# Four layouts for the split operands of a feed-forward: x high and u low in pieces with gaps, x low and u high shifted along their rows

## The chip, the cores and the metric

The kernel runs on one NeuronCore of a Trainium2 chip. Its engines work side by side and meet at semaphores: TensorE (PE, with its weight loads shown apart as PEld), VectorE (DVE), ScalarE (ACT), GpSimd (POOL) and SyncE (SP, which here issues all DMAs). The metric is the device time of one launch in microseconds; lower is better.

## The reference

A linear attention with quadratic features, and behind it a feed-forward with a squared ReLU. Cut to what is computed:

```python
batch, n_heads, seq, head_dim, r = 4, 4, 1088, 32, 8        # all float32

def phi(x):                                       # 64 features from 32 dims
    a = np.einsum('rd,bhsd->bhsr', S1, x)
    b = np.einsum('rd,bhsd->bhsr', S2, x)
    return np.einsum('bhsi,bhsj->bhsij', a, b).reshape(*x.shape[:-1], r * r)
q_p, k_p = phi(q), phi(k)
kv = np.einsum('bhsf,bhsd->bhfd', k_p, v)
z = np.sum(k_p, axis=2)
attn = np.einsum('bhsf,bhfd->bhsd', q_p, kv) / (np.einsum('bhsf,bhf->bhs', q_p, z)[..., None] + 1e-06)

x = attn.transpose(0, 2, 1, 3).reshape(4352, 128)           # tokens x d_model
h = x @ w_in                                                # 128 -> 2048
g = s * np.maximum(h, 0.0) ** 2 + b
out = g @ w_out                                             # 2048 -> 128
```

## The kernel before

The 4352 tokens are the columns of everything: x stands in SBUF as 128 features (partitions) by tokens, and it is cut into nine tiles, one of 256 tokens and eight of 512 (`TILES`, line 26). For each tile the feed-forward runs over eight pairs of 128-wide blocks of the 2048 hidden units (`ffn(t, jp)`, line 527). A pair is two products into one two-bank PSUM tile `hp`, a ReLU and a square on ScalarE (`square`, line 470) that leave `u` in SBUF, and two products that add to the tile's output `ops`.

A float32 product at full precision is made in three passes. Each operand is split in a high part, its value rounded to the type float32r, and a low part, the rest. The weights are split once (`split_weights`, line 448): `wih`, `wil` for w_in and `woh`, `wol` for w_out. The moving operands are split tile by tile: `split_x` (line 257) makes `xh` and `xl` from a tile's attention output, `split_u` (line 477) makes `uh` and `ul` from `u`. In both, the high part is one copy that rounds (line 146, on VectorE or ScalarE by the list `ON_DVE`), and the low part is one VectorE subtraction that reads the value and the high part (lines 263 and 482). A product is then low weights times high stream, high weights times low stream, high times high, in this order, in one PSUM bank (`product`, line 486; each call is a weight load and a matmul that streams 512 columns of the moving operand past the weights). So x high is streamed twice for each block and x low once, u high twice and u low once. The last pair of the last tile makes its second product in two halves of 256 columns, into `psa`.

The first tile of 256 tokens does not split its operands (`first_ffn`, line 494): it multiplies plain float32 tiles. `SPLIT_0 = ((), ())` (line 35) leaves the code for splitting it unused.

The four split tiles lie in SBUF as plain rows of each partition, one float32r after the other: `xh` and `xl` are 512 columns, `uh` and `ul` two times 512. They come from pools with two buffers (`p2`: xh, xl, u) and three (`p3`: uh, ul).

All work is written as generators, one for each load, weight piece, attention tile and feed-forward pair, and a list of names, `ORDER` (line 34), says which of them makes its next step. Each engine runs its instructions in the order in which this list issues them, and nothing is moved afterwards. The change doesn't touch the list.

Of the kernel before, what the change touches and what calls it, by code (L numbers as in the profile page):

```python
# [10 lines left out]
F32R = mybir.dt.float32r  # L11
# [4 lines left out]
ALU = mybir.AluOpType  # L16
# [3 lines left out]
P = 128  # L20
# [4 lines left out]
NMAX = 512  # L25
# [6 lines left out]
VT = 38 * LINE  # L32
EPS = 1e-6
ORDER = """Ls s s z z z z Lq1 Lk0 Lk0 Lv0 Lq0 z Lk0 Lv0 Lw0 z z z z z z z Lv0 Lk1 q1 sr q1 Lcst Lw2 q1 Lk1 Lq2 s k0 k0 k0 k0 p w0 w0 p k0 k0 k0 k0 k0 k0 k0 k0 k0 k1 w0 p k0 k0 k1 w2 w2 k0 k0 z z z z k1 f f f f w0 f Lw3 Lw1 Lv1 q1 Lq3 Lv1 q2 q2 f Lk2 Lw4 Lk2 q1 q1 q1 q1 q2 f k1 f 00 01 k1 k1 w2 w1 w1 w1 w1 w2 00 w3 q3 w3 q3 00 w4 w4 w3 w0 k1 k1 01 k1 k2 02 00 w4 k2 k1 w3 01 w0 k2 w4 k2 k2 02 02 k2 01 03 03 03 Lw6 Lv2 Lv2 Lw5 q2 05 02 04 w1 05 w6 w6 w4 05 q1 n1 n1 n1 n1 n1 w2 03 k2 k2 q3 Lk3 Lw7 Lk3 q2 q2 q2 q2 Lq4 q3 w5 w6 w5 k2 k2 n1 k3 w7 w3 w7 04 04 w6 06 w5 w5 05 n1 n1 06 06 w7 k3 w7 07 04 n1 k1 10 07 07 w2 w4 w1 06 10 10 k3 w5 q2 k1 k1 11 07 11 10 n2 w5 n2 n2 n2 q3 12 10 11 11 11 12 12 n2 n2 k3 q4 13 10 15 11 q3 q3 q3 12 12 q4 n2 n2 w6 w7 13 07 w3 13 15 13 w6 k3 k3 13 12 14 15 15 q3 q4 n2 Lq5 Lv3 Lq6 n2 Lq7 q4 n2 n2 Lv3 17 n3 n3 n3 14 14 n3 14 15 14 q4 q4 n3 q4 n3 07 q4 16 13 15 q7 q5 w7 n2 n2 n2 16 16 q5 16 16 q7 17 17 17 n3 n3 17 14 k2 k3 k3 q5 q5 n3 n3 n3 n3 20 20 16 21 k2 20 k3 21 21 17 23 24 q4 20 20 k2 k3 23 23 21 21 24 n4 n4 n4 n4 23 23 22 20 21 25 n4 24 22 17 22 n4 q5 q5 q5 q5 24 24 23 n4 n4 n3 22 22 n3 25 25 25 n3 25 24 22 26 27 25 q6 q5 q6 n4 n4 n4 q6 26 27 26 26 26 27 n5 n5 n5 n5 27 27 30 30 34 34 34 30 26 34 31 32 27 30 n5 n5 n5 30 34 31 31 32 31 31 n4 q6 17 q6 q6 q6 q6 30 34 33 32 32 32 33 33 33 33 n4 n5 q6 31 36 k3 k3 n4 k3 36 36 36 36 32 33 35 37 n4 35 35 37 27 q7 q7 n5 n5 35 35 n6 n6 n6 37 n6 37 37 q7 Lq8 n5 n6 n5 27 n6 36 40 40 42 35 37 41 40 40 42 40 n5 n6 q7 q7 q7 37 42 41 41 42 42 n6 44 40 43 42 n5 41 41 44 44 43 43 43 n5 44 44 q7 43 45 46 41 q8 q8 n7 46 46 46 46 n7 n7 45 n7 44 43 50 45 50 45 50 45 47 46 q8 n6 q8 n6 n7 n7 50 n7 q8 n6 q8 n6 37 47 47 50 47 n7 47 52 45 51 52 51 52 51 51 50 53 47 52 52 53 n6 51 53 54 54 53 53 52 51 56 54 54 53 55 54 56 56 n6 n6 47 56 55 55 55 q8 q8 56 q8 n7 n7 n7 n7 n7 55 57 54 56 60 n8 47 57 57 n8 60 n8 n8 57 60 57 62 55 61 57 n8 n8 n8 60 62 62 62 60 n8 63 62 60 62 61 57 61 61 61 63 n7 63 64 65 61 64 64 63 n7 63 64 65 65 65 64 66 63 65 66 66 n8 n8 n8 n8 57 66 66 64 67 70 67 67 70 70 67 67 65 71 71 70 70 71 72 66 67 n8 71 71 n8 72 72 72 72 73 74 73 70 71 72 75 74 74 73 73 73 74 74 n8 75 75 75 75 76 73 77 76 76 77 77 81 74 80 76 76 76 75 77 77 81 81 80 80 81 81 82 77 83 82 67 67 80 80 82 83 83 82 82 84 80 81 85 84 84 83 83 85 85 86 82 84 84 87 83 84 85 85 86 77 86 86 86 85 86 87 87 77 86 87 87 87 87 87 87 87 87"""
SPLIT_0 = ((), ())
DIRECT = (1,)
ON_DVE = """a6 a8 b03 b06 b10 b30 b35 d2 d3 d4 k31 n1 n2 n3 n6 n7 n8 u10 u12 u16 u20 u21 u22 u23 u24 u26 u30 u31 u32 u33 u34 u35 u37 u41 u42 u44 u45 u50 u52 u53 u57 u61 u63 u66 u67 u70 u71 u73 u74 u75 u76 u77 u80 u82 u83 u84 u85 u86 u87 w0 w1 w2 w5 w7 x2 x4 x6""".split()
CMASK, CS, CB, CID = 0, 2, 3, 4
# [20 lines left out]
def attn_ffn_kernel(ctx: ExitStack, tc: tile.TileContext, qT, kT, vp, s64, cst, w_in, w_out, outT):  # L59
    nc = tc.nc  # L60
# [3 lines left out]
    p2 = ctx.enter_context(tc.tile_pool(name="p2", bufs=2))  # L64
# [7 lines left out]
    def f32(ap):  # L72
        return ap.bitcast(F32)
# [71 lines left out]
    def copy(key, out, in_):  # L145
        (nc.vector.tensor_copy if key in ON_DVE else nc.scalar.copy)(out=out, in_=in_)  # L146
# [109 lines left out]

    def split_x(t, x):
        N = tiles[t][1] - tiles[t][0]
        xh = p2.tile([P, NMAX], F32R, name="xh")
        xl = p2.tile([P, NMAX], F32R, name="xl")  # L260
        copy(f"x{t}", xh[:, :N], x[:, :N])
        yield
        nc.vector.tensor_tensor(out=xl[:, :N], in0=x[:, :N], in1=f32(xh[:, :N]), op=ALU.subtract)
        xhl[t] = (xh, xl)
        yield

# [29 lines left out]
    def first_attend(t):  # L296
        N = tiles[t][1] - tiles[t][0]
        pq, st = qfeat.pop(t), kv_st[0]
        C = N // P
        nd = ps_h.tile([P, 2, 512], F32, name="hp")  # L300
        for c in range(C):
            for g in range(2):
                nc.tensor.matmul(nd[:, 0, 4 * c + 2 * g:4 * c + 2 * g + 2], pq[:, g, c * P:(c + 1) * P],
                                 st[:, 1 + g, :2], start=(c == 0 and g == 0),
                                 stop=(c == C - 1 and g == 1), skip_group_check=True)
        yield
        rc = const.tile([P, LINE], F32, name="rc0")[:, :4 * C].rearrange("p (c h) -> p c h", h=4)
        nc.vector.tensor_scalar(out=rc, in0=nd[:, 0, :4 * C].rearrange("p (c h) -> p c h", h=4), scalar1=EPS,
                                scalar2=None, op0=ALU.add)
        yield  # L310
        nc.vector.reciprocal(out=rc, in_=rc)
        yield
        rx = const.tile([P, C, P], F32, name="rx")
        for c in range(C):
            nc.vector.tensor_copy(out=rx[:, c].rearrange("p (g d j) -> p g d j", g=2, j=2),
                                  in_=rc[:, c].rearrange("p (g j) -> p g j", g=2).unsqueeze(2).broadcast_to([P, 2, D, 2]))
        yield
        numerators(nd[:, 1, :N], st, pq, slice(0, N))
        yield
        num = const.tile([P, N], F32, name="num0")  # L320
        nc.scalar.copy(out=num, in_=nd[:, 1, :N])
        yield
        rp = ps_a.tile([P, 512], F32, name="psa")
        for c in range(C):
            nc.tensor.matmul(rp[:, c * P:(c + 1) * P], rx[:, c], ident,  # L325
                             start=(c == 0), stop=(c == C - 1), skip_group_check=True)
        yield
        x = const.tile([P, N], F32, name="x0")
        nc.vector.tensor_tensor(out=x, in0=num, in1=rp[:, :N], op=ALU.mult)
        x_first.append(x)  # L330
        yield
        if any(SPLIT_0):
            yield from split_x(t, x)

    def qfeatures(t):
        N = tiles[t][1] - tiles[t][0]
# [138 lines left out]
        return u  # L475

    def split_u(key, u, N):
        uh = p3.tile([P, 2, NMAX], F32R, name="uh")
        copy(key, uh[:, :, :N], u[:, :, :N])
        yield  # L480
        ul = p3.tile([P, 2, NMAX], F32R, name="ul")
        nc.vector.tensor_tensor(out=ul[:, :, :N], in0=u[:, :, :N], in1=f32(uh[:, :, :N]), op=ALU.subtract)  # L482
        yield
        return uh, ul

# [8 lines left out]
    def first_ffn(jp):  # L494
        N = TILES[0]
        hp = ps_h.tile([P, 2, 512], F32, name="hp")
        for i in range(2):
            c, c24 = columns(2 * jp + i)
            if jp in SPLIT_0[0]:
                xh, xl = (x[:, :N] for x in xhl[0])  # L500
                terms = ((wil[:, c], xh), (wih[:, c], xl), (wih[:, c], xh))
            else:
                terms = ((w24[jp // 2, 0][c24], x_first[0]),)
            product(hp[:, i, :N], terms)
        yield
        u = yield from square(hp, N)

        nc.scalar.copy(out=u[:, :, N:N + 2], in_=b_col.unsqueeze(2).broadcast_to([P, 2, 2]))
        yield
        W = N + 2  # L510
        if jp in SPLIT_0[1]:
            uh, ul = yield from split_u(f"u0{jp}", u, W)
        if jp == 0:
            o_ps[0] = ps_o.tile([P, 512], F32, name="ops")
        for i in range(2):
            c, c24 = columns(2 * jp + i)
            if jp in SPLIT_0[1]:
                terms = ((wol[:, c], uh[:, i, :W]), (woh[:, c], ul[:, i, :W]), (woh[:, c], uh[:, i, :W]))
            else:
                terms = ((w24[jp // 2, 1][c24], u[:, i, :W]),)  # L520
            product(o_ps[0][:, :W], terms, jp == i == 0, jp == NPAIR - 1 and i == 1)
        yield
        if jp == NPAIR - 1:
            nc.scalar.copy(out=bias, in_=o_ps[0][:, N:N + 1])
            yield from finish(0, o_ps[0], slice(0, N))

    def ffn(t, jp):
        N = tiles[t][1] - tiles[t][0]
        xh, xl = (x[:, :N] for x in xhl[t])
        hp = ps_h.tile([P, 2, 512], F32, name="hp")  # L530
        for i in range(2):
            c, _ = columns(2 * jp + i)
# [10 lines left out]
        for a in range(2 if final else 1):  # L543
# [2 lines left out]
            o = ps_a.tile([P, 512], F32, name="psa") if final else o_ps[t]  # L546
            for i in range(2):
                c, _ = columns(2 * jp + i)
                product(o[:, :M], ((wol[:, c], uh[:, i, s]), (woh[:, c], ul[:, i, s]), (woh[:, c], uh[:, i, s])),
                        i == 0 and (jp == 0 or final), i == 1 and (last or final))  # L550
            yield
            if final:
# [80 lines left out]
```

## Time and profile before

| what | value |
|---|---|
| median of two runs | 241.64 us (241.63 to 241.65) |
| the profiled execution's own time | 241.36 us |
| its span, first to last instruction | 239.3 us |
| PE busy | 234.9 us (98%) |
| PE weight loads busy | 185.0 us (77%) |
| ACT busy | 190.4 us (80%) |
| DVE busy | 168.6 us (70%) |
| POOL busy | 3.0 us (1%) |
| mean granted TensorE clock | 1.000 |

The profiled execution is 0.28 us shorter than the median, and 2.1 us of it lie outside the span. A matmul's recorded duration reaches past the start of the next one, because matmuls are pipelined and their ends are modelled; how fast they follow each other is read from their starts, or from the chain of waits, which counts each only once. Weight loads are shown beside the matmuls and overlap them.

### The profile page before, as it was taken

Reading aid. Unit: us, or ns where it says so; the run is one execution under the profiler, and the core shown is the slowest. Engines: PE = TensorE matmul, PEld = TensorE weight load, DVE = VectorE, ACT = ScalarE, POOL = GpSimd, SP = SyncE. Lnnn points to the kernel's source line nnn. Section 1 sums busy time; section 2 is a strip of 40 time slices with the busy share of each in tenths; the row PEclk is TensorE's granted clock in tenths of the full one; section 3 lists DMA queues with packets and bytes.
Section 4 is the critical chain, followed back from the end, with each engine's and each line's share of the span. In section 5 each row is a group of like instructions: output and inputs, shape, how many; then the busy total and the mean of one; then the engine's idle time right before and its main releaser. Section 6 shows DMA issues by size and latency. Waiting matters only on the chain.

```text
span 239.3 us, 3880 instructions
## 1 busy us (share of the span) xinstructions
PE 234.9 (98%) x1481; PEld 185.0 (77%) x1482; DVE 168.6 (70%) x224; ACT 190.4 (80%) x238; POOL 3.0 (1%) x16
## 2 busy tenths in 40 slices
PE   8999999999999999999999999999999999999994
PEld 3978869778678786788788778887688888788883
DVE  1677979988777684579868865667655682965973
ACT  3348779799767887968789969999998989697971
POOL 3010000000000000000000000000000000000000
PEclk9999999999999999999999999999999999999999
DMA  6999985057641050252054017002002000000011
GB/s 172 361 405 318 322 297 176 3 133 257 178 135 44 4 169 29 89 130 70 1 184 129 1 53 223 15 0 88 1 4 88 0 0 0 3 0 31 13 45 44
DMA packets 15541, 25.21 MB, mean 105 GB/s; under 512 B 3492, under 2 KB 6052, under 8 KB 15524
## 3 DMA queue, kind: packets, MB, share of 16 engines
q1 hardware_dynamic: 15524, 24.98, 32.6%
q8 instruction: 11, 0.18, 0.3%
q14 instruction: 6, 0.05, 0.1%
HBM read 21.59 MB, written 3.33 MB: 104 GB/s over the span
## 4 chain that ended last, share of the span: by engine, by line
PE 97%; DVE 1%; issue 0%
PE hp L488 40%; PE ops L488 39%; PE psa L221 4%; PE psa L199 3%; PE psa L250 3%; PE ops L578 2%; PE psa L342 2%; PE psa L407 1%; PE hp L286 1%; PE psa L488 1%; DVE ph L206 1%; PE psa L418 0%; PE psa L325 0%; PE hp L250 0%; PE psa L234 0%; DVE ot L553 0%
## 5 line engine op out<-in xcount | busy, mean ns | idle before, releaser
L482 DVE TENSOR_TENSOR ul<-u,uh 128x1024 fp32r<-128x1024 f32 x64 | 78.2, 1224 | 21.4 <-ACT uh L146 19.9
L472 ACT ACTIVATE u<-hp 128x1024 f32<-128x1024 f32 (+1 forms) x72 | 70.2, 976 | 23.3 <-PE hp L488 12.1
L474 ACT ACTIVATE u<-u 128x1024 f32<-128x1024 f32 (+1 forms) x72 | 72.5, 1013 | 1.7
L488 PE MATMUL hp<-xh,wil 128*128 128x512 f32 x128 | 51.1, 399 | 0.0
L488 PE MATMUL hp<-xl,wih 128*128 128x512 f32 x128 | 49.9, 390 | 0.0
L488 PE MATMUL hp<-xh,wih 128*128 128x512 f32 x128 | 49.9, 390 | 0.0
L488 PE MATMUL ops<-uh,wol 128*128 128x512 f32 x126 | 49.5, 393 | 0.0
L488 PE MATMUL ops<-ul,woh 128*128 128x512 f32 x126 | 49.1, 390 | 0.0
L488 PE MATMUL ops<-uh,woh 128*128 128x512 f32 x126 | 49.1, 389 | 0.0
L146 DVE CAST uh<-u 128x1024 fp32r<-128x1024 f32 x42 | 29.0, 692 | 24.9 <-ACT u L474 22.0
L488 PEld LDWEIGHTS hp<-xh,wil 128*128 128x128 f32 x128 | 24.0, 188 | 7.4 <-issue 1.4
L488 PEld LDWEIGHTS ops<-uh,wol 128*128 128x128 f32 x126 | 23.7, 188 | 5.8 <-issue 0.8
L488 PEld LDWEIGHTS hp<-xh,wih 128*128 128x128 f32 x128 | 24.0, 188 | 5.2
L488 PEld LDWEIGHTS hp<-xl,wih 128*128 128x128 f32 x128 | 24.0, 188 | 4.7
L488 PEld LDWEIGHTS ops<-uh,woh 128*128 128x128 f32 x126 | 23.7, 188 | 5.0
L488 PEld LDWEIGHTS ops<-ul,woh 128*128 128x128 f32 x126 | 23.6, 188 | 4.8
L146 ACT CAST uh<-u 128x1024 fp32r<-128x1024 f32 x22 | 23.1, 1049 | 0.6
L206 DVE TENSOR_TENSOR ph<-psa,bk 128x768 f32<-128x768 f32 (+2 forms) x9 | 11.0, 1221 | 3.9 <-ACT bk L146 3.8
L360 DVE TENSOR_TENSOR pq<-pq,br 128x1024 f32<-128x1024 f32 x8 | 9.7, 1211 | 0.0
L199 PEld LDWEIGHTS psa<-sk,kt 128*128 128x128 f32 x72 | 9.0, 191 | 0.9 <-issue 0.4
L199 PE MATMUL psa<-sk,kt 128*128 128x64 f32 x72 | 9.3, 274 | 0.0
L127 ACT ACTIVATE w<-raw 128x512 f32<-128x512 f32 x8 | 5.4, 679 | 4.9 <-DMA raw<-w_in 4.8
(88 smaller groups left out, 176.5 us busy)
## 6 DMA issues: line engine op xcount, KB each, us to landing
pq<-qd SPq DMA_DIRECT2D x16, 256.0 KB
br<-qd SPq DMA_DIRECT2D x16, 256.0 KB
qt<-qT SPq DMA_DIRECT2D x8, 256.0 KB
raw<-w_in SPq DMA_DIRECT2D x4, 512.0 KB
raw<-w_out SPq DMA_DIRECT2D x4, 512.0 KB
rr<-rd SPq DMA_DIRECT2D x14, 128.0 KB
outT<-ot SPq DMA_DIRECT2D x7, 256.0 KB
qd<-abq SPq DMA_DIRECT2D x16, 64.0 KB
```

Source lines behind the costliest of these rows:

```text
L127: nc.scalar.activation(out=out, in_=high.bitcast(F32), func=AF.Abs, scale=2.0 ** -112)
L146: (nc.vector.tensor_copy if key in ON_DVE else nc.scalar.copy)(out=out, in_=in_)
L199: nc.tensor.matmul(av[:, :, i, :], kt[:, (c0 + i) * P:(c0 + i + 1) * P], sk.rearrange("p (w x) -> p w x", w=2), start=(i == 0), stop=(i == ...
L206: nc.vector.tensor_tensor(out=ph[:, c0:c0 + n].rearrange("p c h i x -> p (c h) i x"), in0=a[:, :n * 32].rearrange("p (g y) -> p g y", y=R) ...
L221: nc.tensor.matmul(kvp[64 * g:64 * g + VW, 64 * j:64 * j + 64], v_in[b][:, c, h], ph[:, c, h].rearrange("p i x -> p (i x)"), start=(c == 0 ...
L250: nc.tensor.matmul(out[r:r + 32], st[:, 3 * g, r % 64:r % 64 + 32], pq[:, g, cols], start=True, stop=True, skip_group_check=True)
L342: nc.tensor.matmul(ab[r:r + 32, :M], sq[:, r % 64:r % 64 + 32], qT_t[t][:, a * M:(a + 1) * M], start=True, stop=True, skip_group_check=True)
L360: nc.vector.tensor_tensor(out=pq[:, :, :N], in0=pq[:, :, :N], in1=br[:, :, :N], op=ALU.mult)
L472: nc.scalar.activation(out=u[:, :, :N], in_=hp[:, :, :N], func=AF.Relu)
L474: nc.scalar.activation(out=u[:, :, :N], in_=u[:, :, :N], func=AF.Square)
L482: nc.vector.tensor_tensor(out=ul[:, :, :N], in0=u[:, :, :N], in1=f32(uh[:, :, :N]), op=ALU.subtract)
L488: nc.tensor.matmul(out, w, x, start=(first and k == 0), stop=(last and k == len(terms) - 1), skip_group_check=True)
```

## The change

Each of the four streams gets a layout of its own in SBUF; their values, the instructions and their order stay.

- `xh`: the tile is twice as long, 64 groups of two times 8 elements, and the second 8 of each group are used. The stream is 64 pieces of 32 bytes with 32 bytes between them, and it begins 32 bytes into the tile.
- `xl`: a plain row that begins 4 elements (16 bytes) into a tile 32 elements longer.
- `uh`: two plain rows of 512 that begin 12 elements (48 bytes) into rows of 544.
- `ul`: two rows of 16 groups of two times 32 elements, of which the first 32 are used: pieces of 128 bytes with 128 bytes between them.

The access patterns of the copies that write the high parts, of the subtractions that read these and write the low parts, and of the matmuls that stream all four follow; no DMA reads or writes these tiles. In `ffn` a stream's slice of the last pair counts `ul` in groups of 32. The unused `SPLIT_0` code goes.

```diff
     def split_x(t, x):
         N = tiles[t][1] - tiles[t][0]
-        xh = p2.tile([P, NMAX], F32R, name="xh")
-        xl = p2.tile([P, NMAX], F32R, name="xl")
-        copy(f"x{t}", xh[:, :N], x[:, :N])
-        yield
-        nc.vector.tensor_tensor(out=xl[:, :N], in0=x[:, :N], in1=f32(xh[:, :N]), op=ALU.subtract)
+
+        xh = p2.tile([P, NMAX // 8, 2, 8], F32R, name="xh")[:, :, 1]
+        xl = p2.tile([P, NMAX + 32], F32R, name="xl")[:, 4:NMAX + 4]
+        copy(f"x{t}", xh, x.rearrange("p (g c) -> p g c", c=8))
+        yield
+        nc.vector.tensor_tensor(out=xl.rearrange("p (g c) -> p g c", c=8), in0=x.rearrange("p (g c) -> p g c", c=8),
+                                in1=f32(xh), op=ALU.subtract)
         xhl[t] = (xh, xl)
         yield
...
     def split_u(key, u, N):
-        uh = p3.tile([P, 2, NMAX], F32R, name="uh")
-        copy(key, uh[:, :, :N], u[:, :, :N])
-        yield
-        ul = p3.tile([P, 2, NMAX], F32R, name="ul")
-        nc.vector.tensor_tensor(out=ul[:, :, :N], in0=u[:, :, :N], in1=f32(uh[:, :, :N]), op=ALU.subtract)
+
+        uh = p3.tile([P, 2, NMAX + 32], F32R, name="uh")[:, :, 12:NMAX + 12]
+        copy(key, uh, u)
+        yield
+        ul = p3.tile([P, 2, NMAX // 32, 2, 32], F32R, name="ul")[:, :, :, 0]
+        nc.vector.tensor_tensor(out=ul, in0=u.rearrange("p i (g c) -> p i g c", c=32),
+                                in1=f32(uh).rearrange("p i (g c) -> p i g c", c=32), op=ALU.subtract)
         yield
         return uh, ul
...
     def ffn(t, jp):
         N = tiles[t][1] - tiles[t][0]
-        xh, xl = (x[:, :N] for x in xhl[t])
+        xh, xl = xhl[t]
...
-                product(o[:, :M], ((wol[:, c], uh[:, i, s]), (woh[:, c], ul[:, i, s]), (woh[:, c], uh[:, i, s])),
+                product(o[:, :M], ((wol[:, c], uh[:, i, s]), (woh[:, c], ul[:, i, s.start // 32:s.stop // 32]), (woh[:, c], uh[:, i, s])),
                         i == 0 and (jp == 0 or final), i == 1 and (last or final))
```

No instruction changes its place on any engine. VectorE's queue where the third tile's attention output is split (`xh`, `xl`) between feed-forward pairs (`uh`, `ul`), before:

```order
L435 TENSOR_TENSOR rr<-num,rr 128x512
L146 CAST xh<-rr 128x512
L263 TENSOR_TENSOR xl<-rr,xh 128x512
L146 CAST uh<-u 128x1024
L482 TENSOR_TENSOR ul<-u,uh 128x1024
```

and the same place now:

```order
L434 TENSOR_TENSOR rr<-num,rr 128x512
L145 CAST xh<-rr 128x64x8
L263 TENSOR_TENSOR xl<-rr,xh 128x512
L145 CAST uh<-u 128x2x512
L482 TENSOR_TENSOR ul<-u,uh 128x32x32
```

The shapes of the written tiles are split up, and the numbers of lines differ by the deleted ones; the rest reads the same.

More of the change, by code (lines that the diff above doesn't have):

```diff
@@ L34 @@
 ORDER = """Ls s s z z z z Lq1 Lk0 Lk0 Lv0 Lq0 z Lk0 Lv0 Lw0 z z z z z z z Lv0 Lk1 q1 sr q1 Lcst Lw2 q1 Lk1 Lq2 s k0 k0 k0 k0 p w0 w0 p k0 k0 k0 k0 k0 k0 k0 k0 k0 k1 w0 p k0 k0 k1 w2 w2 k0 k0 z z z z k1 f f f f w0 f Lw3 Lw1 Lv1 q1 Lq3 Lv1 q2 q2 f Lk2 Lw4 Lk2 q1 q1 q1 q1 q2 f k1 f 00 01 k1 k1 w2 w1 w1 w1 w1 w2 00 w3 q3 w3 q3 00 w4 w4 w3 w0 k1 k1 01 k1 k2 02 00 w4 k2 k1 w3 01 w0 k2 w4 k2 k2 02 02 k2 01 03 03 03 Lw6 Lv2 Lv2 Lw5 q2 05 02 04 w1 05 w6 w6 w4 05 q1 n1 n1 n1 n1 n1 w2 03 k2 k2 q3 Lk3 Lw7 Lk3 q2 q2 q2 q2 Lq4 q3 w5 w6 w5 k2 k2 n1 k3 w7 w3 w7 04 04 w6 06 w5 w5 05 n1 n1 06 06 w7 k3 w7 07 04 n1 k1 10 07 07 w2 w4 w1 06 10 10 k3 w5 q2 k1 k1 11 07 11 10 n2 w5 n2 n2 n2 q3 12 10 11 11 11 12 12 n2 n2 k3 q4 13 10 15 11 q3 q3 q3 12 12 q4 n2 n2 w6 w7 13 07 w3 13 15 13 w6 k3 k3 13 12 14 15 15 q3 q4 n2 Lq5 Lv3 Lq6 n2 Lq7 q4 n2 n2 Lv3 17 n3 n3 n3 14 14 n3 14 15 14 q4 q4 n3 q4 n3 07 q4 16 13 15 q7 q5 w7 n2 n2 n2 16 16 q5 16 16 q7 17 17 17 n3 n3 17 14 k2 k3 k3 q5 q5 n3 n3 n3 n3 20 20 16 21 k2 20 k3 21 21 17 23 24 q4 20 20 k2 k3 23 23 21 21 24 n4 n4 n4 n4 23 23 22 20 21 25 n4 24 22 17 22 n4 q5 q5 q5 q5 24 24 23 n4 n4 n3 22 22 n3 25 25 25 n3 25 24 22 26 27 25 q6 q5 q6 n4 n4 n4 q6 26 27 26 26 26 27 n5 n5 n5 n5 27 27 30 30 34 34 34 30 26 34 31 32 27 30 n5 n5 n5 30 34 31 31 32 31 31 n4 q6 17 q6 q6 q6 q6 30 34 33 32 32 32 33 33 33 33 n4 n5 q6 31 36 k3 k3 n4 k3 36 36 36 36 32 33 35 37 n4 35 35 37 27 q7 q7 n5 n5 35 35 n6 n6 n6 37 n6 37 37 q7 Lq8 n5 n6 n5 27 n6 36 40 40 42 35 37 41 40 40 42 40 n5 n6 q7 q7 q7 37 42 41 41 42 42 n6 44 40 43 42 n5 41 41 44 44 43 43 43 n5 44 44 q7 43 45 46 41 q8 q8 n7 46 46 46 46 n7 n7 45 n7 44 43 50 45 50 45 50 45 47 46 q8 n6 q8 n6 n7 n7 50 n7 q8 n6 q8 n6 37 47 47 50 47 n7 47 52 45 51 52 51 52 51 51 50 53 47 52 52 53 n6 51 53 54 54 53 53 52 51 56 54 54 53 55 54 56 56 n6 n6 47 56 55 55 55 q8 q8 56 q8 n7 n7 n7 n7 n7 55 57 54 56 60 n8 47 57 57 n8 60 n8 n8 57 60 57 62 55 61 57 n8 n8 n8 60 62 62 62 60 n8 63 62 60 62 61 57 61 61 61 63 n7 63 64 65 61 64 64 63 n7 63 64 65 65 65 64 66 63 65 66 66 n8 n8 n8 n8 57 66 66 64 67 70 67 67 70 70 67 67 65 71 71 70 70 71 72 66 67 n8 71 71 n8 72 72 72 72 73 74 73 70 71 72 75 74 74 73 73 73 74 74 n8 75 75 75 75 76 73 77 76 76 77 77 81 74 80 76 76 76 75 77 77 81 81 80 80 81 81 82 77 83 82 67 67 80 80 82 83 83 82 82 84 80 81 85 84 84 83 83 85 85 86 82 84 84 87 83 84 85 85 86 77 86 86 86 85 86 87 87 77 86 87 87 87 87 87 87 87 87"""
-SPLIT_0 = ((), ())
@@ L331, in first_attend @@
         yield
-        if any(SPLIT_0):
-            yield from split_x(t, x)
     def qfeatures(t):
@@ L498, in first_ffn @@
             c, c24 = columns(2 * jp + i)
[L499 to L503, printed above, removed]
+            terms = ((w24[jp // 2, 0][c24], x_first[0]),)
             product(hp[:, i, :N], terms)
@@ L510, in first_ffn @@
         W = N + 2
-        if jp in SPLIT_0[1]:
-            uh, ul = yield from split_u(f"u0{jp}", u, W)
         if jp == 0:
@@ L516, in first_ffn @@
             c, c24 = columns(2 * jp + i)
[L517 to L520, printed above, removed]
+            terms = ((w24[jp // 2, 1][c24], u[:, i, :W]),)
             product(o_ps[0][:, :W], terms, jp == i == 0, jp == NPAIR - 1 and i == 1)
```

## The prediction

> **What bounds the kernel now.** The page comes first: its span, the busy shares, the clock, and the chain of work that ended last.
>
> ```profile
> span 239.3 us, 3880 instructions
> ...
> PE 234.9 (98%) x1481; PEld 185.0 (77%) x1482; DVE 168.6 (70%) x224; ACT 190.4 (80%) x238; POOL 3.0 (1%) x16
> ...
> PEclk9999999999999999999999999999999999999999
> ...
> PE 97%; DVE 1%; issue 0%
> PE hp L488 40%; PE ops L488 39%; PE psa L221 4%; PE psa L199 3%; PE psa L250 3%; PE ops L578 2%; PE psa L342 2%; PE psa L407 1%; PE hp L286 1%; PE psa L488 1%; DVE ph L206 1%; PE psa L418 0%; PE psa L325 0%; PE hp L250 0%; PE psa L234 0%; DVE ot L553 0%
> ```
>
> TensorE is the bound from end to end, at a clock that is granted in full, and four fifths of the chain are line 488, the feed-forward's products. The view of waits, for PE alone, says whether anything makes it wait:
>
> ```profile
> PE ops L578 <- PEq L625: 0.8, 1, 0.8
> PE hp L250 <- DVE rc L308: 0.3, 1, 0.3
> ```
>
> Two waits, 1.1 us in all, both in the first 16 us. The feed-forward never waits for its operands. So what counts first is how fast its matmuls follow each other. The groups by line and shape give their number:
>
> ```profile
> L488 PE MATMUL hp<-xh,wil 128*128 128x512 f32 x128 | 51.1, 399 | 0.0
> L488 PE MATMUL hp<-xl,wih 128*128 128x512 f32 x128 | 49.9, 390 | 0.0
> L488 PE MATMUL hp<-xh,wih 128*128 128x512 f32 x128 | 49.9, 390 | 0.0
> L488 PE MATMUL ops<-uh,wol 128*128 128x512 f32 x126 | 49.5, 393 | 0.0
> L488 PE MATMUL ops<-ul,woh 128*128 128x512 f32 x126 | 49.1, 390 | 0.0
> L488 PE MATMUL ops<-uh,woh 128*128 128x512 f32 x126 | 49.1, 389 | 0.0
> ```
>
> That is 256 streams of x high, 128 of x low, 252 of u high and 126 of u low: 762. Their durations (390 ns) overlap; the pace is in the chain, in order of time (start, us, what):
>
> ```profile
> 24.71 0.87 PE ops L488 x4
> ...
> 50.43 1.60 PE hp L488 x6
> ...
> 54.78 2.72 PE ops L488 x12
> 57.50 2.72 PE hp L488 x12
> ```
>
> Undisturbed, twelve take 2.72 us, 226.7 ns each, x streams and u streams alike. 762 times 226.7 ns is 172.7 us, 72% of the span: a nanosecond on each is 0.76 us. The first row is the first tile's plain float32 product: four records of 258 columns in 0.87 us, 217.5 ns each, the fastest full-length pace in these rows. How the 226.7 ns split up shows in the last pair, which streams 256 columns at a time (timeline, start and duration in us):
>
> ```profile
> 234.87 0.28 PE L488 MATMUL psa<-uh,wol 128*128 128x256 f32 x1
> ...
> 235.82 0.28 PE L488 MATMUL psa<-uh,woh 128*128 128x256 f32 x1
> ```
>
> Eight intervals in 0.95 us, 118.8 ns each. So 256 more columns cost 226.7 - 118.8 = 107.9 ns, 0.42 ns a column, and some 11 ns per matmul don't grow with the columns. And just after another kind of work (the 1.60 us above) the same streams run slower for a while:
>
> ```profile
> 50.70 0.40 PE L488 MATMUL hp<-xl,wih 128*128 128x512 f32 x1
> 50.94 0.40 PE L488 MATMUL hp<-xh,wih 128*128 128x512 f32 x1
> 51.18 0.40 PE L488 MATMUL hp<-xh,wil 128*128 128x512 f32 x1
> 51.41 0.40 PE L488 MATMUL hp<-xl,wih 128*128 128x512 f32 x1
> 51.65 0.39 PE L488 MATMUL hp<-xh,wih 128*128 128x512 f32 x1
> ```
>
> Four intervals in 0.95 us are 237.5 ns, 10.8 above the settled pace, with the same layout. The pace is thus not a constant of the columns; something in how loads and streams meet is worth 10 ns either way.
>
> **The change, part by part.** Nothing is added, removed or moved: every engine issues the same instructions in the same order, on the same queues, and no DMA touches the four tiles. Only addresses change, so there are three prices: reading the streams on TensorE, and writing them on VectorE and ScalarE.
>
> *The streams on TensorE.* All four layouts are read with whole runs of at least eight columns. No row of this profile shows a float32r stream with gaps or with a shifted start, so the price is bounded. Below: 217.5 ns, the pace of the float32 rows, is 9.2 ns less, 7.0 us over 762. Above, for the shifted starts: the disturbed pace, +10.8 ns, on 128 + 252 = 380 streams 4.1 us. Above, for the gaps: if what lies between the pieces were fetched too, x high's streams would take twice the time, +226.7 ns on 256, 58.0 us. I take zero: a stream that delivers its columns in order from 32-byte or longer runs is nearest to the plain one in the rows, and the two shifted streams are plain rows but for their first address.
>
> [...]
>
> *Writing and re-reading them.* The rows, from the groups of VectorE and ScalarE:
>
> ```profile
> L482 DVE TENSOR_TENSOR ul<-u,uh 128x1024 fp32r<-128x1024 f32 x64 | 78.2, 1224 | 21.4 <-ACT uh L146 19.9
> L146 DVE CAST uh<-u 128x1024 fp32r<-128x1024 f32 x42 | 29.0, 692 | 24.9 <-ACT u L474 22.0 <-PE ops L488 2.8
> L263 DVE TENSOR_TENSOR xl<-rr,xh 128x512 fp32r<-128x512 f32 x8 | 5.5, 687 | 0.2
> L130 DVE SCALAR_TENSOR_TENSOR w<-raw,w 128x512 int32<-128x512 int32 x8 | 5.4, 686 | 0.1
> L146 DVE CAST xh<-rr 128x512 fp32r<-128x512 f32 x3 | 1.3, 421 | 0.0
> ...
> L146 ACT CAST uh<-u 128x1024 fp32r<-128x1024 f32 x22 | 23.1, 1049 | 0.6
> L127 ACT ACTIVATE w<-raw 128x512 f32<-128x512 f32 x8 | 5.4, 679 | 4.9 <-DMA raw<-w_in 4.8
> L146 ACT CAST xh<-rr 128x512 fp32r<-128x512 f32 x5 | 3.1, 618 | 1.5 <-DVE rr L435 1.5
> ```
>
> Line 130 reads every second word of `raw` (4 bytes, a 4-byte gap) and takes 686 ns, the plain subtraction of line 263 takes 687: gaps cost VectorE's two-input instructions nothing. Line 127 reads the same words on ScalarE in 679 ns against 618 ns of a plain copy, at most 61 ns per 512 columns: 22 copies of 1024 and 5 of 512 give 3.0 us more on an engine that is idle for 20% of 239.3 us, 48 us. VectorE's copies are the open term. They move 1024 columns in 692 ns where the subtraction needs 1224, so they take two at a time. If the split shape made them go one at a time, 42 copies times 532 ns and 3 times 266 ns are 23.1 us more, and DVE would be busy 192 us, 80%. The cover is the time between a subtraction's end and the matmul that reads it. It is thin at places (VectorE's row, then PE's):
>
> ```profile
> 107.49 1.23 DVE L482 TENSOR_TENSOR ul<-u,uh 128x1024 fp32r<-128x1024 f32 x1
> ...
> 108.98 0.40 PE L488 MATMUL ops<-ul,woh 128*128 128x512 f32 x1
> ```
>
> The low part is ready at 108.72 and streamed from 108.98 on: 0.26 us. A copy that is 0.53 us later makes PE wait 0.27 us there. Bounds of that case: 0.27 us if this place alone is so tight, 42 x 0.27 = 11.3 us if all were. The new shapes keep the same count in the same order, so I take zero here too.
>
> *The sum*: 241.36 us of the profiled execution plus nothing. On the median of the runs, 0.28 us above it, 241.6 us.
>
> **The rivals.**
>
> *A, gaps are fetched* (slower). x high's 256 streams double: 241.6 + 58.0 = 299.6 us; if 128-byte pieces double as well, 126 x 226.7 ns = 28.6 us on top. For it: a stream that takes a column each 0.42 ns leaves no visible slack. Against it: nothing in the rows reads ahead. Chance 0.09.
>
> *B, each piece costs a step* (slower; the mechanism on the other side). If the stream loses one column's time, 0.42 ns, at each start of a piece, x high's 64 pieces cost 27.0 ns, 6.9 us over 256 streams, and u low's 16 pieces 6.7 ns, 0.85 us over 126: 249.4 us. Two columns' time: 257.1 us. It decides from 4.8 us on, the 2% that a measurement of this kernel tells from no change: 18.9 ns per stream of x high, 0.3 ns a piece. For it: the 11 ns per matmul that don't grow with the columns show that starting something costs. Chance 0.16.
>
> *C, the shifted starts cost* (within 2% or slower). Streams that begin 16 or 48 bytes on are held at the disturbed pace: +4.1 us, 245.7 us; if the shift of two streams keeps the other two from settling, +10.8 ns on all 762, 8.2 us, 249.8 us. For it: the 237.5 ns above. Against: that pace dies out within a dozen matmuls. Chance 0.11, of which 0.05 beyond 2%.
>
> *D, the streams get out of the loads' way* (faster). Each stream runs beside the weight load of the next, and now all four begin at the start of their tiles. If part of the 11 ns is the two meeting at the same places in SBUF, shifted or spread streams may meet less: at 217.5 ns on all, 234.6 us. For it: the pace varies with how they stand to each other. Against: it would have to help all four streams. Chance 0.11, of which 0.10 beyond 2%.
>
> *E, VectorE's copies lose their double pace*: between 0.3 and 11.3 us, nearer the lower end, since the view of waits shows PE with no wait behind VectorE; 3 us, 244.6 us. Chance 0.06.
>
> **How the numbers follow.** The forecast, no change, has 0.47; the rivals A 0.09, B 0.16, C 0.11, D 0.11, E 0.06. Slower by over 2%: A, B and 0.05 of C, 0.30. Faster by over 2%: 0.10. Within: 0.60. The likeliest case alone holds 241.0 to 242.5 us. The range leaves out A and nearly all of D, some 0.18, and takes in B up to two columns' time: 238.5 to 257.5 us.
>
> **What would show it.** In the changed kernel's chain the undisturbed runs of twelve matmuls should again take 2.72 us. Each stream has its own rows, so the timeline gives each layout its own price, from one start to the next: 227 ns after x high, x low, u high and u low if I am right; 254 ns after x high alone is B, over 400 is A, 237 after x low and u high is C, 218 is D. E shows in the copies of `uh` at some 1.2 us on VectorE, and in waits of PE for the subtraction, which the view of waits does not have now. The prediction falls if any stream's interval moves by more than 6.3 ns on all, or x high's alone by 18.9.

## The result, and the profile after

The changed kernel takes 245.25 us (median of two runs, 245.24 to 245.26) where the one before takes 241.64: 1.015 times as long, with a 95% interval of 1.011 to 1.019. It is slower by 3.6 us, inside 2% and clear of no change.

The page of the changed kernel: its span, its busy shares, and the engines of the chain that ended last.

```profile
span 243.2 us, 3881 instructions
PE 239.0 (98%) x1482; PEld 185.7 (76%) x1482; DVE 168.8 (69%) x224; ACT 190.7 (78%) x238; POOL 3.0 (1%) x16
PE 97%; DVE 1%; issue 0%
```

TensorE is the bound as before. It waits for the same two things as before, by the view of waits for PE:

```profile
PE ops L570 <- PEq L617: 0.8, 1, 0.8
PE hp L249 <- DVE rc L309: 0.3, 1, 0.3
```

and the instructions that write the streams take what they took. From the groups of VectorE and ScalarE (count, then busy us and mean ns):

```profile
L482 DVE TENSOR_TENSOR ul<-u,uh 128x1024 fp32r<-128x1024 f32 x64 | 78.2, 1224 | 21.1 <-ACT uh L145 19.6
L145 DVE CAST uh<-u 128x1024 fp32r<-128x1024 f32 x42 | 29.0, 691 | 27.3 <-ACT u L473 21.6 <-PE ops L489 4.7 <-PE hp L489 0.8
L145 DVE CAST xh<-rr 128x512 fp32r<-128x512 f32 x3 | 1.3, 421 | 0.0
L145 ACT CAST uh<-u 128x1024 fp32r<-128x1024 f32 x22 | 23.0, 1047 | 0.6
```

What has changed is the pace of the matmuls. The chain of waits in order of time (start, us, what), two undisturbed runs of twelve:

```profile
178.67 2.80 PE ops L489 x12
181.47 2.76 PE hp L489 x12
```

They took 2.72 us before, 226.7 ns each; in these two it is 233 ns for the u streams (`ops`) and 230 for the x streams (`hp`). Taken from one matmul's start to the next one's over the whole profile (intervals over 260 ns left out, where other work lies between), the means by stream are, in ns:

| stream, its layout now | before | after |
|---|---|---|
| x high, 32-byte pieces | 227.5 | 231.9 |
| x low, 16 bytes on | 227.6 | 232.2 |
| u high, 48 bytes on | 227.3 | 232.1 |
| u low, 128-byte pieces | 227.3 | 235.1 |

Times their 241, 128, 245 and 126 such intervals the differences are 3.8 us. With the intervals over 260 ns counted too, all 762 take 3.6 us more, so the loss is here. (The spans of the two profiled executions differ by 3.9 us; some 0.5 us of that lie ahead of the first split product, which starts at 41.71 us instead of 41.25. In e15 and e16 below it starts at 41.72 and 41.87 us, and they lose next to nothing.)

### The profile page after: what moved, and what is told of

Its sections match the earlier page's. It is cut to its first block, busy times and chain, and to the rows that moved or that the text cites. A ratio compares the mean times of both kernels' runs of the same rounds, so it can differ in the third digit from the quotient of the medians.

```text
span 243.2 us, 3881 instructions
## 1 busy us (share of the span) xinstructions
PE 239.0 (98%) x1482; PEld 185.7 (76%) x1482; DVE 168.8 (69%) x224; ACT 190.7 (78%) x238; POOL 3.0 (1%) x16
## 4 chain that ended last, share of the span: by engine, by line
PE 97%; DVE 1%; issue 0%
PE hp L489 40%; PE ops L489 39%; PE psa L220 4%; PE psa L198 3%; PE psa L249 3%; PE ops L570 2%; PE psa L341 2%; PE psa L406 1%; PE hp L287 1%; PE psa L489 1%; DVE ph L205 1%; PE psa L417 0%; PE psa L326 0%; PE hp L249 0%; PE psa L233 0%; DVE ot L545 0%
## 5 line engine op out<-in xcount | busy, mean ns | idle before, releaser
L482 DVE TENSOR_TENSOR ul<-u,uh 128x1024 fp32r<-128x1024 f32 x64 | 78.2, 1224 | 21.1 <-ACT uh L145 19.6
L489 PE MATMUL ops<-ul,woh 128*128 128x512 f32 x126 | 50.2, 398 | 0.0
L489 PE MATMUL ops<-uh,woh 128*128 128x512 f32 x126 | 49.9, 396 | 0.0
L145 ACT CAST uh<-u 128x1024 fp32r<-128x1024 f32 x22 | 23.0, 1047 | 0.6
L558 ACT ACTIVATE ot<-ops,bias,cst_sb 128x512 f32<-128x512 f32 (+1 forms) x9 | 6.7, 749 | 2.9 <-PE ops L489 2.8
```

The source lines that it names most:

```text
L482: nc.vector.tensor_tensor(out=ul, in0=u.rearrange("p i (g c) -> p i g c", c=32), in1=f32(uh).rearrange("p i (g c) -> p i g c", c=32), op=A ...
L489: nc.tensor.matmul(out, w, x, start=(first and k == 0), stop=(last and k == len(terms) - 1), skip_group_check=True)
L558: nc.scalar.activation(out=ot[:, s], in_=o[:, :N], func=AF.Identity, scale=s_col, bias=bias)
```

## The experiments

All kernels start from the one before; the streams and weights that a diff doesn't name lie as before. The diffs show the tiles; the access patterns of the instructions that write them follow. The mean intervals by stream, taken as above from the one profiled execution, and the median times; a ratio with its 95% interval stands where a kernel was run several times, the others ran once:

| run | x high | x low | u high | u low | us | before beside it | ratio |
|---|---|---|---|---|---|---|---|
| e1 x high in pieces | 231.2 | 232.2 | 228.2 | 228.2 | 243.59 | 241.96 | 1.007 (1.005 to 1.009) |
| e2 x low 16 on | 229.6 | 232.8 | 228.5 | 228.7 | 243.59 | 241.96 | 1.006 (1.004 to 1.008) |
| e3 u high 48 on | 228.1 | 228.6 | 230.5 | 230.5 | 243.16 | 241.96 | 1.005 (1.003 to 1.007) |
| e4 u low in pieces | 229.9 | 230.5 | 231.8 | 235.0 | 244.51 | 241.96 | 1.010 (1.008 to 1.012) |
| e5 all streams 16 on | 231.8 | 232.7 | 230.7 | 231.4 | 245.01 | 242.02 | 1.011 (1.008 to 1.014) |
| e6 all streams 64 on | 231.3 | 231.2 | 231.2 | 227.8 | 244.26 | 242.02 | 1.009 (1.006 to 1.011) |
| e7 weights 16 on | 232.2 | 231.4 | 232.2 | 231.4 | 245.21 | 242.02 | 1.014 (1.010 to 1.017) |
| e8 half load | 229.0 | 230.1 | 228.8 | 228.3 | 242.42 | 242.02 | |
| e9 longer rows alone | 232.1 | 231.4 | 230.5 | 231.3 | 244.11 | 241.96 | 1.008 (1.005 to 1.011) |
| e10 streams 16 on, places kept | 231.6 | 231.9 | 231.5 | 231.6 | 245.04 | 241.96 | 1.012 (1.008 to 1.015) |
| e11 weights 16 on, places kept | 233.1 | 232.5 | 232.9 | 232.1 | 245.25 | 241.96 | 1.014 (1.010 to 1.017) |
| e12 both 16 on | 230.6 | 230.5 | 230.5 | 230.4 | 244.13 | 241.96 | 1.009 (1.006 to 1.013) |
| e13 streams 128 on | 233.0 | 232.9 | 233.0 | 233.2 | 245.93 | 241.65 | |
| e14 weights 128 on | 233.0 | 232.4 | 233.0 | 232.7 | 245.77 | 241.65 | |
| e15 both 128 on | 227.3 | 227.6 | 227.1 | 227.5 | 241.80 | 241.65 | |
| e16 streams 256 on | 227.3 | 228.0 | 227.1 | 227.7 | 241.98 | 241.65 | |
| e17 the change, places kept | 231.7 | 231.5 | 233.5 | 234.5 | 245.74 | 242.00 | 1.015 (1.013 to 1.017) |
| e18 x high in pieces from the start | 233.0 | 231.5 | 229.4 | 230.1 | 244.31 | 242.00 | 1.009 (1.007 to 1.011) |

### One layout at a time

e1 takes the change's lines for x high alone, e2 for x low, e3 for u high, e4 for u low:

```diff
# e1
-        xh = p2.tile([P, NMAX], F32R, name="xh")
+        xh = p2.tile([P, NMAX // 8, 2, 8], F32R, name="xh")[:, :, 1]
# e2
-        xl = p2.tile([P, NMAX], F32R, name="xl")
+        xl = p2.tile([P, NMAX + 32], F32R, name="xl")[:, 4:NMAX + 4]
# e3
-        uh = p3.tile([P, 2, NMAX], F32R, name="uh")
+        uh = p3.tile([P, 2, NMAX + 32], F32R, name="uh")[:, :, 12:NMAX + 12]
# e4
-        ul = p3.tile([P, 2, NMAX], F32R, name="ul")
+        ul = p3.tile([P, 2, NMAX // 32, 2, 32], F32R, name="ul")[:, :, :, 0]
```

Expected:

> Only x high lies in 32-byte pieces; x low, u high and u low are plain rows as before. Theory OWN (each layout has a price on its own streams): the two x high matmuls go from 226.7 to about 231 ns, x low and the u streams stay at 226.7; 256 x 4.5 ns = 1.1 us, 242.8 us. Theory MEET (a matmul's pace comes from how its stream and the weight load running beside it get to SBUF, so a changed stream also alters the pace of its neighbours): x low, plain and between two x high matmuls, leaves 226.7 too, the u products far from it stay; about 1.5 to 1.7 us, 243.2 us.

> Only x low begins 16 bytes on. OWN: x low's 128 matmuls at about 232 ns, the rest at 226.7; 0.7 us, 242.3 us. MEET: the x high matmuls beside it change as well; if all 384 x matmuls go to 231, 1.7 us, 243.3 us.

> Only u high begins 48 bytes on. OWN: u high's 252 matmuls at 230 to 235 ns, u low and the x streams at 226.7; about 1.5 us, 243.1 us. MEET: u low, plain, slows too; 378 x 6 ns = 2.3 us, 243.9 us.

> Only u low lies in 128-byte pieces. OWN: u low's 126 matmuls at 234 ns, the rest at 226.7; 0.9 us, 242.5 us. MEET: u high beside it slows too, though it is plain; 378 x 6 ns = 2.3 us, 243.9 us. If 128-byte pieces are free: 241.6 us and 226.7 ns everywhere, and what u low showed in the changed kernel came from u high's shift.

Each costs 0.5 to 1.0%, and the four ratios add up to 2.8% where the four together cost 1.5%. So the layouts have no prices of their own that could be summed. In e1 x low, a plain row, is slowed from 227.6 to 232.2 ns, as much as x high itself; in e3 and e4 the plain u stream is slowed with the other. That is MEET. Neither theory had that in e4 the plain x streams, too, go from 227.5 to 230 ns and more: by the starts in the trace a disturbed stretch takes up to some ten matmuls to come back to 227 ns (eleven in the kernel before, from 50.70 us on), and after six or twelve x matmuls, which from 100 us on take 1.37 to 1.39 and 2.73 to 2.77 us, the u products come again. Over the run of before beside them, e1, e2 and e4 lost 1.6, 1.6 and 2.6 us where MEET's expectations stand 1.6, 1.7 and 2.3 us over 241.6; e3 lost 1.2 us, less than both theories had. In e2 the means hide a stretch that looks as OWN has it. The chain of waits late in e2:

```profile
177.74 2.72 PE ops L485 x12
180.46 2.75 PE hp L485 x12
```

The u streams have settled at 2.72 us and the x streams need 0.03 us more, 7 ns for each of the four x low among the twelve; elsewhere in e2 twelve take up to 2.80. (In this stretch x low lies 144 bytes on, not 16: its longer rows put some of its tiles 128 bytes further, of which more below.) And the 128-byte pieces, the mildest of the four layouts to look at, cost most.

### Streams, or loads

```diff
# e5 (and e6 with 16 for 4), for xh, xl, uh, ul alike
-        xl = p2.tile([P, NMAX], F32R, name="xl")
+        xl = p2.tile([P, NMAX + 32], F32R, name="xl")[:, 4:NMAX + 4]
# e7, for wih, wil, woh, wol alike
-    wih = const.tile([P, DFF], F32R, name="wih")
+    wih = const.tile([P, DFF + LINE], F32R, name="wih")[:, 4:DFF + 4]
# e8
-            product(hp[:, i, :N], ((wil[:, c], xh), (wih[:, c], xl), (wih[:, c], xh)))
+            product(hp[:, i, :N], ((wil[:, c], xh),), last=False)
+            product(hp[:P // 2, i, :N], ((wih[:, c.start:c.start + P // 2], xl),), first=False, last=False)
+            product(hp[:, i, :N], ((wih[:, c], xh),), first=False)
```

> All four streams are plain rows that begin 16 bytes on. Theory START (a stream that doesn't begin on a line of 32 bytes or more costs about 7 ns by itself, as x low did): all 762 matmuls at some 233 ns, 5 us more, 247 us. Theory NEIGHBOUR (only a difference between one stream's layout and the next one's costs): 226.7 ns everywhere, 241.6 us. Theory LOADS (what counts is how a stream stands to the weight load beside it): all streams alike at one new pace, anywhere from 218 to 240 ns.

> All four streams begin 64 bytes on. START with a line of 64 bytes or less: 226.7 ns, 241.6 us; with a line of 128 bytes: 233 ns, 247 us. NEIGHBOUR: 226.7 ns. LOADS: a new pace if places 64 bytes apart differ for SBUF, otherwise 226.7.

> The streams are plain as before; the four split weight tiles begin 16 bytes on. START and NEIGHBOUR: the streams' pace stays at 226.7 ns, 241.6 us, unless the loads themselves take longer than 226 ns (their 188 ns would have to grow). LOADS: the pace changes, in the same way as where all streams are shifted, by up to 10 ns either way (234 to 250 us).

> Plain layouts; the middle pass of the first product (x low) loads only 64 of its 128 weight columns, so it computes half of its outputs: the low part of x is left out for the upper 64 of each block. Its load is half as long. LOADS: the matmul that streams while the half load runs (x high with the low weights) gets faster than 226.7 ns, by up to half of the 11 ns that don't grow with the columns, to some 221 ns. START and NEIGHBOUR: no interval changes, 226.7 ns.

e7 decides: the streams are as before, only the weights have moved, and every stream's mean goes to 231 to 232 ns. START and NEIGHBOUR, which look at the streams alone, fall with it. So a stream's pace depends on where the load beside it reads. (`LINE` is 32 elements, so each weight tile is 128 bytes longer, and the low ones lie 144 bytes on in steps of 256; e5 and e6 have a second move of this kind in them. The next runs take it apart for 16 bytes; 64 bytes alone were not run. e7's profiled execution took 246.66 us, and its first split product starts 2.3 us later than before: its paces count here, not that time.) But not as LOADS had it in e8: the load of x low's pass is shorter, though not half as long,

```profile
L485 PEld LDWEIGHTS hp<-xl,wih 128*64 128x64 f32 x128 | 17.2, 134 | 4.8
```

134 ns where the others take 188, and the matmul that runs beside it (x high with the low weights) takes 228 ns to the next start, not 221; the x streams around it lose their settled pace instead, 230 ns after x low. A shorter load did not make the stream beside it faster. (This is read off one trace; its time, 242.42 us, lies among the 241.49 to 242.70 us of the runs of before beside it.)

### Places, in which steps

The shifted runs hid a second move: rows that are 32 elements longer put the next tile, and the second row of a u tile, 128 bytes further on. e9 has the longer rows without any shift; e10 to e12 shift by 16 bytes with rows longer by 512 bytes.

```diff
# e9, for xh, xl, uh, ul alike
+        xl = p2.tile([P, NMAX + 32], F32R, name="xl")[:, :NMAX]
# e10, for the four streams
+        xl = p2.tile([P, NMAX + 128], F32R, name="xl")[:, 4:NMAX + 4]
# e11, for the four weight tiles
+    wih = const.tile([P, DFF + 128], F32R, name="wih")[:, 4:DFF + 4]
# e12: both
```

> The streams start where their tiles start, as before, but their rows are 32 elements longer, as in the runs with shifted streams: the tiles and the second rows of u high and u low thereby move by multiples of 128 bytes against each other and against the weights. If the 16, 48 or 64 bytes of the shifts are what counts, nothing changes: 226.7 ns, 241.6 us. If places 128 bytes apart differ too (theory PLACE, any move of a stream against the load beside it counts), the pace is unsettled as with the shifts: 229 to 233 ns, 243.5 to 246 us, and the shifts of the earlier runs were not alone in what they did.

> All four streams begin 16 bytes on, with rows longer by 128 elements (512 bytes), so that every tile keeps its place in steps of 512 bytes. A start of 16 bytes off against the loads: 231 to 234 ns, some 245 us. If the 128-byte moves did it in the earlier run with all streams 16 bytes on: 226.7 ns.

> The four split weight tiles begin 16 bytes on, longer by 512 bytes, all places otherwise kept; streams plain. Theory LOADS (place of stream against load): the pace leaves 226.7 ns, 231 to 234, some 245 us. If only moves by 128 bytes count: 226.7 ns, 241.6 us.

> Streams and weight tiles all begin 16 bytes on, places otherwise kept: the place of each stream against each load is the one of before. LOADS as a matter of their places against each other: back at 226.7 ns and 241.6 us. If a start off the line costs each of them by itself: the slowest of all, 233 ns and more, 246 us or above.

The longer rows alone cost 0.8%: PLACE, and a warning, since every shift before had this in it. With places kept, 16 bytes on the streams or on the loads each still cost over 1%; in e10 all four streams lie alike, which NEIGHBOUR had at 226.7 ns, and run at 231.6 to 231.9. Both together came out between the two expectations: neither back at 226.7 nor slowest. The chain of waits, e11 and then e12:

```profile
178.30 2.80 PE ops L485 x12
181.10 2.80 PE hp L485 x12
```

```profile
177.88 2.76 PE ops L485 x12
180.64 2.76 PE hp L485 x12
```

The means of e7 and e11 hide a second thing. The chain of waits in e11 from 82.9 us on, and in e7 from 145.4 us on:

```profile
82.90 2.72 PE ops L485 x12
91.06 2.72 PE hp L485 x12
```

```profile
145.35 2.72 PE hp L485 x12
158.96 2.72 PE ops L485 x12
```

With the loads moved the streams can still run at 226.7 ns, for 58 matmuls in e11 and 124 in e7, and after the next piece of other work the same kernel is back at 2.80 us. So the places don't fix the pace by themselves; what decides between the two paces was not tested. What the places change is how much of the time the pace is settled. Runs of at least twelve intervals of 224 to 229 ns hold 608 of the 762 before, 178 in e7, 58 in e11, and none in e10, in e12 and in the changed kernel.

At 128 bytes the four cases were run once more, and 256 bytes beside them.

```diff
# e13, for the four streams
+        xl = p2.tile([P, NMAX + 128], F32R, name="xl")[:, 32:NMAX + 32]
# e14, for the four weight tiles
+    wih = const.tile([P, DFF + 128], F32R, name="wih")[:, 32:DFF + 32]
# e15: both; e16: the streams with 64 for 32
```

> All four streams begin 128 bytes on, tiles otherwise kept in steps of 512 bytes. PLACE (any move of a stream against the load beside it counts, in steps of 128 bytes too): the settled 226.7 ns goes, 229 to 234 ns on all, some 244 us. If 128 bytes matter only where the streams differ from each other, as in the run with longer rows: 226.7 ns, 241.8 us.

> The four split weight tiles begin 128 bytes on, streams plain. PLACE: as with the streams moved, 229 to 234 ns, some 244 us. [...]

> Streams and loads both begin 128 bytes on. If the place of one against the other is what counts: back at 226.7 ns and 241.8 us. If each one's own place counts (as it looked where both began 16 bytes on): not 226.7, 229 to 232 ns, some 244 us.

> All four streams begin 256 bytes on. In the run with x low 16 bytes on, the u streams stood 256 bytes further on than before and kept 226.7 ns, so 256 bytes should not count: 226.7 ns, 241.8 us. If they do: 229 to 234 ns.

The chain of waits, in this order e13, e14, e15, e16:

```profile
179.10 2.80 PE ops L485 x12
181.90 2.80 PE hp L485 x12
```

```profile
179.00 2.80 PE ops L485 x12
181.80 2.80 PE hp L485 x12
```

```profile
176.28 2.72 PE ops L485 x12
179.00 2.72 PE hp L485 x12
```

```profile
176.49 2.72 PE ops L485 x12
179.21 2.72 PE hp L485 x12
```

This is the clear case, though each ran once. Streams 128 bytes on: twelve take 2.80 us, and the kernel is 4.3 us slower. Loads 128 bytes on: 2.80 us again, 4.1 us slower. Both: 2.72 us, as if nothing had been moved. Streams 256 bytes on: 2.72 us again. Runs of twelve at 224 to 229 ns hold 613 of the 762 matmuls in e15 and 624 in e16, and none in e13 and e14. So for moves of plain rows by 128 bytes it is the place of stream against load that counts, and a difference of 256 bytes is none. e12 shows that this is not the whole rule: there, too, streams and loads have moved alike, and the pace is 230.5 ns. In the kernel before, by the addresses that building it gives, every stream and every load starts at a whole multiple of 256 bytes.

### What is left of the change

```diff
# e17: the changed kernel, with rows longer by 256 bytes instead of 128
-        xl = p2.tile([P, NMAX + 32], F32R, name="xl")[:, 4:NMAX + 4]
+        xl = p2.tile([P, NMAX + 64], F32R, name="xl")[:, 4:NMAX + 4]
-        uh = p3.tile([P, 2, NMAX + 32], F32R, name="uh")[:, :, 12:NMAX + 12]
+        uh = p3.tile([P, 2, NMAX + 64], F32R, name="uh")[:, :, 12:NMAX + 12]
# e18: e1 with the first 8 elements of each 16 for the second
-        xh = p2.tile([P, NMAX], F32R, name="xh")
+        xh = p2.tile([P, NMAX // 8, 2, 8], F32R, name="xh")[:, :, 0]
```

> The four layouts of the change, but x low and u high get rows longer by 256 bytes instead of 128, so that no tile and no second row moves by 128 bytes against the loads: what is left are the starts 16, 32 and 48 bytes on and the gaps. If the 128-byte moves are a good part of the change's loss: clearly under it, 242.5 to 244 us. If starts and gaps do it alone: 245.2 us, paces of 230 to 235 ns as in the change.

> Only x high in 32-byte pieces, as in the first experiment, but the first 8 of each 16 are used, so the stream begins at its tile's start and not 32 bytes on. If the start was what unsettled the x streams: 226.7 ns and 241.8 us. If the gaps do (the stream then passes the places in SBUF at twice the rate of the load): 230 to 231 ns on all x streams again, 243.5 us.

Taking the 128-byte moves away saves nothing: 1.015 against 1.015. And x high's pieces cost 0.9% when they begin at the load's own place (0.7% in e1, 32 bytes on). The chain of waits, e18:

```profile
186.66 2.73 PE ops L486 x12
189.39 2.79 PE hp L486 x12
```

The gaps alone unsettle the x streams, as those of u low, which begins at its tile's start, do in e4. Why they do is not shown. The reason given in the expectation, that a stream with gaps passes the places at twice the load's rate, does not fit the rows: 64 columns more of a load take 54 ns (134 and 188 ns in e8), by estimate 0.84 ns a column, and a stream takes a column each 0.42 ns. A plain stream, too, passes at about twice the load's rate, and it settles. That the loads have a part in the price of the gaps was not tested either.

So the change loses its 3.6 us because each of its layouts, shifts and gaps alike, keeps the streams from settling at 226.7 ns for most of the time (the runs of at least twelve at 224 to 229 ns hold 70, 101, 60 and none of the 762 matmuls in e1 to e4, and 608 before), and once they are out of it, at 230 to 235 ns, a second and third layout add little. No layout that was run is faster than the kernel before; e15 and e16 equal it.

## Why the prediction was wrong

**What bounds the kernel** held: TensorE from end to end, no new wait, and a nanosecond on 762 streams worth 0.76 us.

**The streams on TensorE, taken as zero**, is the step that failed. Its reason was that order and runs of 32 bytes and more make a stream as good as a plain one. Measured, the four streams went up by 4.4, 4.6, 4.8 and 7.8 ns, 3.8 us. The bounds held (217.5 to 237.5 ns for starts; nothing near twice the time for gaps), though the lower one was read from records of 258 float32 columns and not, as it says, from full-length ones. What was wrong was to put the value at the settled pace of plain rows, which no row showed for another layout, although the rows showed the same plain streams between 226.7 and 237.5 ns. In e14 the streams are untouched and slow down, so what a stream looks like by itself does not settle its pace. The signs that it named failed with it: twelve matmuls take up to 2.80 us and no stream stays at 227 ns. Its limit for falling, 6.3 ns on all streams, was too wide to notice 3.6 us.

**Writing and re-reading at zero**, and with it rival E: right. 1224, 691, 421 and 1047 ns against 1224, 692, 421 and 1049, and PE waits for none of them. That VectorE's copies take two columns at a time is the prediction's estimate, from rows in which 512 more columns cost a copy 271 ns and the subtraction 537.

**Rival A** (gaps are fetched) and **rival B** (each piece costs a step) are excluded: x high follows at 232 ns, not at over 400 or at 254; u low, with a quarter of x high's pieces, costs more than x high.

**Rival C** comes nearest. That a shift of two streams keeps the others from settling was there, with 249.8 us if all 762 stay at 237.5; they stay at 232 to 235, half of it, and not for the shifted starts alone: the gaps do it too. That its first case, 245.7 us, is so near the measured 245.25 is luck: it has 380 streams at 237.5 ns and the others unchanged.

**Rival D** had the right two partners for plain rows, stream and load, and the wrong sign: starting alike (before, e15, e16) is the best that was found, not what to get out of.

**The numbers**: the likeliest case's own range, 241.0 to 242.5 us, missed by 2.7 us. The 0.60 for within 2% held, and so did the wide range, but by its width, which was drawn for rival B.

## What to carry to other kernels

Where TensorE streams back to back with a new weight load beside each matmul, the start of the moving tile and that of the stationary tile counted together here: plain rows whose starts are alike in steps of 256 bytes, both on whole 128 bytes, kept 226.7 ns (before, e15, e16). Starts alike but both 16 bytes on cost 0.9% (e12), and the moves of one against the other that were run cost up to 1.8% (e13), a move by a neighbour's padding 0.8% (e9). When a trace shows one instruction at two paces with nothing else changed, a change of its operands' places has no zero in it until a run says so. And a control that has the side effect alone (here the longer rows) belongs beside each layout that is tried.

## What was not expected of the hardware

Moving only the stationary operand by 128 bytes (e14) slowed all moving streams by about 5 to 6 ns, 4.1 us in all, and the loads themselves took 188 ns as before. The loads of x low's pass, before and in e14:

```profile
L488 PEld LDWEIGHTS hp<-xl,wih 128*128 128x128 f32 x128 | 24.0, 188 | 4.7
L485 PEld LDWEIGHTS hp<-xl,wih 128*128 128x128 f32 x128 | 24.1, 188 | 5.4
```

Out of the settled relation the pace in e13 and e12 is not one number but a short cycle that repeats. In e13 it is two: by the starts in the trace, matmuls follow each other at 237 to 238 and 229 to 230 ns in turn, for x and u streams alike (twelve in 2.80 us); in e12 at 232 and 228 (twelve in 2.76 us). Why both 16 bytes on does not restore what both 128 bytes on does, what lets e7 and e11 settle in some stretches and not in others, which steps under 128 bytes count, why gaps cost, and how the place of the loads comes to act on the streams, stays open.
